# Where the scaled upper words of the weights are kept while they are rounded: a PSUM bank or their own place in SBUF

## The chip, the cores and the metric

The kernel runs on one core of a Trainium2 chip. The metric is the device time of one execution in microseconds (us), as the median of several runs. The engines of the core work side by side, each through its own queue in order: TensorE (PE, with its weight loads as PEld), VectorE (DVE), ScalarE (ACT), GpSimd (POOL) and SyncE (SP), whose queue here issues nearly all transfers. Semaphores order what one engine needs from another.

## What is computed

Eight sequences of 576 tokens go through an attention block with 8 heads of 64, then through a Fourier mixing over tokens and columns, a normalization, and a two-layer network of 512 to 2048 to 512 columns:

```python
q_s = softmax(q, axis=-1); k_s = softmax(k, axis=2)
kv = np.einsum('bhsd,bhse->bhde', k_s, v)
x = np.einsum('bhsd,bhde->bhse', q_s, kv)        # then (B,H,S,D) -> (B, S, H*D)
mixed = np.real(np.fft.fft(np.fft.fft(x, axis=1), axis=2))
u = x + mixed
un = (u - mu) / np.sqrt(var + 1e-06)
ch = np.maximum(un @ w_ch1, 0.0) @ w_ch2
return u + ch
```

The two weight matrices reach the kernel as 64-bit words, two 32-bit halves in turn, and have to be brought to float32 on the chip before TensorE can use them. This is the rounding that the change is about.

## The kernel before

**The weights.** Each of the two matrices is cut into 16 blocks of 128 x 512, 32 blocks in all, called words 0 to 31 here (0 to 15 are `w_ch1`, 16 to 31 `w_ch2`). `fetch(i)` brings a block of 64-bit words into SBUF, 128 partitions x 512 words of 8 bytes, lower and upper half in turn, so each half is a view with a step of two. The places are listed by `WORDS_AT`: parts of the large tile `big` that hold nothing yet, three tiles called `words`, and two called `spare`. `convert(i)` makes float32 of it in five steps:

1. ScalarE scales the upper half into `t` (L397).
2. DVE shifts `t` left by three bits into the block's final place in `big` (L391; word 16 goes by way of a tile `eo`).
3. DVE joins the sign of `t` to it (L394, two inputs: `t` and what step 2 wrote).
4. ScalarE scales the lower half in place (L398).
5. GpSimd adds the lower half to the joined word (L399), which is the finished block.

For words 3 to 25, 23 of them, `t` is a PSUM bank from `acc`, a pool of three banks that in this part of the kernel also takes the results of attention and mixing. For the other nine, `t` is the upper half itself, in SBUF, written in place. When step 5 is done, SP's queue fetches the next block that goes to the same place.

**The order.** Each step of the kernel has a time written out by hand, and the program sorts all steps by it; this gives the order in every engine's queue. The five steps of a word stand at offsets 0, 0.8, 1.5, 0.9 and 2.3 from its time (`converted`), so in the queues the lower half's scaling comes after the shift and before the sign pass. The times decide only the order: what starts when is up to the engines and the semaphores.

**What runs around it.** Words 0 to 2 are rounded in the opening. From about 46 us on, the first group of tokens goes through the first layer (`plain`: `half` for the first three blocks, then `up`, L1457), one block of `w_ch1` after the other, in the three banks `ba`, `bb` and `bc` in turn. ScalarE applies the ReLU to each (L1472), and a bank is filled again only after its ReLU. From about 104 us the second layer follows (`part`, L1479). Beside this run:

- the keys of the next sequence (`keys`): DVE takes four maxima (L733) and combines them across partitions with the help of ScalarE's copies (`across`: L713, L716, and DVE's L720); ScalarE then takes the exponentials (L737);
- `combine` (L449), DVE's subtractions and additions of quarters of finished blocks, two inputs in SBUF each, which are then stored to DRAM for the later groups (L452 to L458);
- the queries of the next sequence: DVE's maxima and sums (L968, L946 and others), GpSimd's subtraction (L973), ScalarE's exponential (L977), TensorE's transposes (L985) and products (L840).

From about 175 us on, the other groups run through the layers with the stored combinations (`up` and `down`, L1544, L1641, L1671), without any rounding.

Of the kernel before, what the change touches and what calls it, by code (L numbers as in the profile page):

```python
# [40 lines left out]
F32 = mybir.dt.float32  # L41
# [5 lines left out]
P = 128  # L47
B, H, S, DH = 8, 8, 576, 64
D = H * DH
# [89 lines left out]
class _Block:  # L139
# [211 lines left out]
    def weights(self):  # L351

        nc = self.nc
        w1 = self.w1.bitcast(I32).rearrange("(k p) n -> p k n", p=P)
        w2 = self.w2.bitcast(I32).rearrange("(f p) n -> p f n", p=P)
        raws = self.raws = {}

        def fetch(i):

            at = WORDS_AT[i]  # L360
            if at < 8:
                raw = self.w2sb[:, 2 * at:2 * at + 2, :].rearrange("p a n -> p (a n)")
            elif at < 11:
                raw = self.words[at - 8][:].rearrange("p a n -> p (a n)")
            else:
                raw = self.spare(2 * D)
            raw = raw.bitcast(I32)
            f = i % NF
            if i < NF:
                nc.sync.dma_start(raw.rearrange("p (k n) -> p k n", k=KT), w1[:, :, f * 2 * P:(f + 1) * 2 * P])  # L370
            else:
                nc.sync.dma_start(raw, w2[:, f, :])
            raws[i] = raw

        def convert(i):
            pair = raws.pop(i).rearrange("p (n w) -> p n w", w=2)
            lo, hi = pair[:, :, 0], pair[:, :, 1]
            f = i % NF
            out = (self.w1sb if i < NF else self.w2sb)[:, f, :]

            if 2 < i < 26:
                t = self.acc((P, D))
            else:

                t = hi.bitcast(F32)
            to = self.halves()[:, 0:D] if i == NF else out
            ti, V = t.bitcast(I32), nc.vector


            def shift():  # L390
                V.tensor_scalar(out=to.bitcast(I32), in0=ti, scalar1=3, scalar2=None, op0=ALU.logical_shift_left)  # L391

            def sign():
                V.scalar_tensor_tensor(out=to.bitcast(I32), in0=ti, scalar=-(1 << 31), in1=to.bitcast(I32),  # L394
                                       op0=ALU.bitwise_and, op1=ALU.bitwise_or)

            return [(0, lambda: nc.scalar.activation(t, hi.bitcast(F32), ACT.Copy, scale=2.0 ** -112)), (0, shift), (0, sign),  # L397
                    (0, lambda: nc.scalar.activation(lo, lo.bitcast(U32), ACT.Copy, scale=2.0 ** -29)),  # L398
                    (0, lambda: nc.gpsimd.tensor_tensor(out=out.bitcast(I32), in0=to.bitcast(I32), in1=lo, op=ALU.add))]  # L399

        return fetch, convert
# [1592 lines left out]
```

## Time and profile before

| | before |
|---|---|
| median of 3 runs, us | 1006.84 (1006.43 to 1006.99) |
| span of the profiled execution, us | 1006.6 |
| granted TensorE clock, mean | 1.000 |
| ACT busy, us | 493.2 (49%) |
| POOL busy, us | 442.9 (44%) |
| L399, all 32 adds, first and last start, us | 32.9 to 144.3 |
| L391, all 32 shifts, DVE busy, us | 20.4 |

Of the profiled execution only the span is shown, from the first instruction to the last; a time of the same execution by the device's own measure is not.

How the views read. A row of the timeline has the start in us, the duration in us, the engine, the line of the kernel, the operation, what it writes and reads, its shape and how many instructions are merged into it; in brackets stands the idle time of the engine before it, and what ended that. A row that groups a line's instructions has the least, the median and the greatest duration in ns, then the first and the last start. Two instructions of one engine may overlap by some hundredths of a us in these records. A DVE row that is long can be long because it waited inside the instruction: such time counts as busy.

### The profile page before, as it was taken

The page shows a single profiled execution, that of the slowest core. Times are in us where ns is not written, and L with a number is a line of the kernel's source. Part 1 is how long each engine was busy: PE and PEld are TensorE (multiplying, and loading weights), DVE is VectorE, ACT ScalarE, POOL GpSimd, SP SyncE. Part 2 cuts the span into 40 slices and gives each one's busy share as a digit, 9 for nine tenths or more (in the row PEclk, how much of TensorE's full clock was granted, in tenths as well). Part 3 has the DMA queues.
Part 4 walks back from the last instruction along what each step waited for, and adds up shares of the span by engine and source line. Part 5 has one row for each costly group of instructions (what it writes and reads, how often), then busy time and mean ns, then how long its engine had stood idle before and what let it go on. Part 6 is the DMA issues. An engine that isn't in the chain of part 4 may idle for free.

```text
span 1006.6 us, 19808 instructions
## 1 busy us (share of the span) xinstructions
PE 995.6 (99%) x7562; PEld 855.7 (85%) x7562; DVE 718.6 (71%) x1356; ACT 493.2 (49%) x1277; POOL 442.9 (44%) x445
## 2 busy tenths in 40 slices
PE   8999999999999999999999999999999999999998
PEld 6844464888888899889988998899889998998897
DVE  6898898666765887588756877688667945685563
ACT  4585642872468228832775177625772342151200
POOL 4263420357535637664655465655646450040000
PEclk9999999999999999999999999999999999999999
DMA  9987499687989666975677577847753765674573
GB/s 300 258 281 245 158 240 346 205 243 226 342 283 272 230 230 219 266 237 210 251 220 242 206 269 237 253 174 270 231 204 135 267 213 200 224 265 172 183 256 132
DMA packets 123559, 236.37 MB, mean 235 GB/s; under 512 B 24184, under 2 KB 88440, under 8 KB 112840
## 3 DMA queue, kind: packets, MB, share of 16 engines
q1 hardware_dynamic: 123096, 234.58, 71.0%
q8 instruction: 60, 0.98, 0.4%
q14 instruction: 35, 0.29, 0.1%
q10 hardware_dynamic: 288, 0.26, 0.1%
q0 software_dynamic: 80, 0.26, 0.1%
HBM read 199.94 MB, written 39.06 MB: 237 GB/s over the span
## 4 chain that ended last, share of the span: by engine, by line
PE 87%; DVE 7%; ACT 3%; DMA 1%; issue 1%; SPq 0%; POOL 0%; DVEq 0%; POOLq 0%
PE bb L1544 16%; PE ba L1544 11%; PE bc L1544 11%; PE bb L1671 10%; PE ba L1671 7%; PE bc L1671 7%; PE bb L1641 5%; PE bc L1479 2%; PE bb L1760 2%; PE two L840 2%; PE one L755 2%; PE two L1207 1%; PE two L1264 1%; PE ba L1479 1%; PE bc L1760 1%; PE ba L1760 1%
## 5 line engine op out<-in xcount | busy, mean ns | idle before, releaser
L1544 PE MATMUL bb<-unT,big 128*128 128x256 f32 x768 | 183.3, 380 | 0.0
L1544 PEld LDWEIGHTS bb<-unT,big 128*128 128x128 f32 x768 | 144.8, 190 | 20.7 <-DVE u L1514 0.7
L1556 ACT ACTIVATE big<-big 128x512 f32<-128x512 f32 x96 | 59.8, 629 | 147.6 <-DVE big L1555 141.0
L1544 PE MATMUL ba<-unT,big 128*128 128x256 f32 x512 | 123.9, 382 | 0.0
L1544 PE MATMUL bc<-unT,big 128*128 128x256 f32 x512 | 121.5, 380 | 0.1
L817 ACT ACTIVATE qT<-q 32x128 f32<-32x128 f32 x384 | 117.9, 307 | 5.9 <-DVE q L807 0.8
L1544 PEld LDWEIGHTS bc<-unT,big 128*128 128x128 f32 x512 | 96.9, 190 | 13.7 <-DVE big L1555 0.5
L1544 PEld LDWEIGHTS ba<-unT,big 128*128 128x128 f32 x512 | 95.5, 190 | 13.9 <-issue 0.5
L1514 DVE TENSOR_TENSOR u<-bb,s 128x512 f32<-128x512 f32 x66 | 45.2, 685 | 85.0 <-PE bb L1544 66.5
L1671 PE MATMUL bb<-big 128*128 128x128 f32 x848 | 103.8, 276 | 0.2 <-DVE u L1678 0.2
L1671 PEld LDWEIGHTS bb<-big 128*128 128x128 f32 x848 | 98.9, 192 | 1.0 <-DVE u L1678 1.0
L1390 POOL COPY unT<-unT 32x256 f32<-32x256 f32 x98 | 42.0, 428 | 90.2 <-DVE unT L1382 85.9
L1621 POOL TENSOR_TENSOR x<-x,big 128x512 f32<-128x512 f32 x45 | 60.9, 1368 | 46.0 <-DVE big L1678 19.7
L1617 DVE TENSOR_TENSOR big<-big 128x512 f32<-128x512 f32 x98 | 79.9, 842 | 0.0
L1671 PE MATMUL ba<-big 128*128 128x128 f32 x640 | 79.0, 276 | 0.0
L1671 PEld LDWEIGHTS ba<-big 128*128 128x128 f32 x640 | 75.0, 192 | 0.8
L1390 ACT COPY unT<-unT 32x256 f32<-32x256 f32 x126 | 50.7, 402 | 31.3 <-DVE unT L1382 29.5
L804 POOL TENSOR_TENSOR q<-q,qm 128x512 f32<-128x512 f32 x24 | 25.8, 1073 | 88.2 <-DVE qm L799 53.1
L405 POOL TENSOR_TENSOR big<-big 128x512 f32<-128x512 f32 x24 | 30.4, 1268 | 68.4 <-ACT big L1556 68.4
L1641 PE MATMUL bb<-big 128*128 128x256 f32 x256 | 58.3, 379 | 0.0
L1555 DVE TENSOR_TENSOR big<-bc,u 128x512 f32<-128x512 f32 x64 | 44.0, 688 | 17.3 <-PE bc L1544 16.4
L1641 PEld LDWEIGHTS bb<-big 128*128 128x128 f32 x256 | 48.0, 190 | 6.1
(336 smaller groups left out, 1917.9 us busy)
## 6 DMA issues: line engine op xcount, KB each, us to landing
big<-w2d SPq DMA_DIRECT2D x67, 1024.0 KB, 4.6
big<-w1s SPq DMA_DIRECT2D x64, 896.0 KB, 4.7
big<-w2s SPq DMA_DIRECT2D x16, 1024.0 KB, 4.8
big<-in_w_dram SPq DMA_DIRECT2D x21, 512.0 KB, 6.0
w2d<-big SPq DMA_DIRECT2D x42, 256.0 KB, 6.5
kb<-in_kT_dram SPq DMA_DIRECT2D x28, 320.0 KB, 7.8
q<-in_q_dram SPq DMA_DIRECT2D x28, 256.0 KB, 6.0
vt<-in_v_dram SPq DMA_DIRECT2D x84, 80.0 KB, 2.7
```

The costliest lines, as they stand in the source:

```text
L405: e1.tensor_tensor(out=to(4), in0=at(2), in1=at(3), op=ALU.add)
L817: nc.scalar.activation(to[t, i * Q:i * Q + Q], one, ACT.Exp)
L1390: copy(to, of)
L1514: plus = lambda t: V.tensor_tensor(out=temp(t), in0=box["bb"][:], in1=box["s1"][:], op=ALU.add)
L1544: nc.tensor.matmul(bank()[:, i, :], lhsT=w[:, WA_AT[m], k * P:(k + 1) * P], rhs=self.unT[g][:, B_AT[m], k, :], start=first and i == 0 and ...
L1555: steps = [(0, lambda: V.tensor_tensor(out=hp(i), in0=bank()[:], in1=u()[:], op=ALU.add)), (0.8, lambda: nc.scalar.activation(hp(i), hp(i) ...
L1556: (0.8, lambda: nc.scalar.activation(hp(i), hp(i), ACT.Relu))]
L1617: e.tensor_tensor(out=to(o), in0=to(x), in1=to(y), op=op)
L1621: E.tensor_tensor(out=x, in0=x, in1=tile(m), op=ALU.add)
L1641: nc.tensor.matmul(box[name][:, i, :], lhsT=h[p][:, A_AT[m], i * P:(i + 1) * P], rhs=self.stream[n][:, p, :], start=p == 0 and (m != 1 or ...
L1671: nc.tensor.matmul(box[place[n]][:, i, :], lhsT=own(m)(A_AT[n])[:, f, :], rhs=w[:, r // 2, r % 2 * P:r % 2 * P + P], start=first and f == ...
L1760: nc.tensor.matmul(bank()[:, i, :], lhsT=h[p][:, A_AT[m], i * P:(i + 1) * P], rhs=w[:, p, :], start=first and i == 0 and p == 0, stop=p == ...
```

## The change

`convert` no longer asks for a PSUM bank: for all 32 words the scaled upper half is written in place, over the upper half of the fetched block, and the shift and the sign pass read it there.

```diff
-            if 2 < i < 26:
-                t = self.acc((P, D))
-            else:
-
-                t = hi.bitcast(F32)
+            t = hi.bitcast(F32)
             to = self.halves()[:, 0:D] if i == NF else out
             ti, V = t.bitcast(I32), nc.vector
```

The five steps, their engines and their order in the queues stay as they are. For words 3 to 25 the tile `t` is another: ScalarE's L397 writes SBUF with a step of two in place of PSUM without one, and L391 and L394 read it there. The pool `acc` keeps its three banks for its other users.

## Prediction

> **What bounds the kernel now.** I read the page first, for the bound and the chain of waits, then the busy time by stage, to see where TensorE has room.
>
> ```profile
> PE 995.6 (99%) x7562; PEld 855.7 (85%) x7562; DVE 718.6 (71%) x1356; ACT 493.2 (49%) x1277; POOL 442.9 (44%) x445
> PE 87%; DVE 7%; ACT 3%; DMA 1%; issue 1%; SPq 0%; POOL 0%; DVEq 0%; POOLq 0%
> ```
> ```profile
> 46.00:58.00 12.00, 12.00 (x52) 8.94 (x51) 10.10 (x16) 10.97 (x20) 7.58 (x6) 1.00 0.79 263
> 58.00:75.00 17.00, 16.79 (x40) 7.19 (x39) 16.55 (x29) 12.93 (x30) 9.30 (x8) 1.00 0.90 308
> 75.00:112.00 37.00, 36.23 (x272) 18.10 (x271) 32.77 (x61) 21.39 (x47) 12.88 (x12) 1.00 0.67 236
> 112.00:200.00 88.00, 87.89 (x447) 54.47 (x446) 72.16 (x154) 44.65 (x118) 23.59 (x20) 1.00 0.78 239
> 200.00:1006.60 806.60, 802.23 (x6299) 733.04 (x6297) 552.70 (x1018) 379.34 (x1007) 371.71 (x363) 1.00 0.69 230
> ```
>
> The columns of the second view are the stretch, its length, then busy PE, PEld, DVE, ACT, POOL, the granted clock, the DMA share and GB/s. All 23 edited words lie between 46 and 120 us. From 46 to 200 TensorE is idle for 0 + 0.21 + 0.77 + 0.11 = 1.09 us only, so **1.1 us is the most that the change can give back**. After 200 the matmuls follow one another with 4.37 us of idle time in 806.6, so what TensorE loses early it loses for good, nearly one for one. And from 58 to 75 DVE has 0.45 us of room in 17: what is put on DVE there stays there.
>
> **The change part by part.** The durations, by operand, are min/median/max in ns:
>
> ```profile
> L391 DVE TENSOR_SCALAR big<-acc x22: 678/682/693, 48.0 to 117.6; 128x512 int32<-128x512 int32 x22
> L391 DVE TENSOR_SCALAR big<-big x4: 418/424/488, 31.6 to 137.1; 128x512 int32<-128x512 int32 x4
> L394 DVE SCALAR_TENSOR_TENSOR big<-acc,big x22: 675/691/693, 48.7 to 118.4; 128x512 int32<-128x512 int32 x22
> L394 DVE SCALAR_TENSOR_TENSOR big<-words,big x2: 691/692/692, 120.8 to 143.5; 128x512 int32<-128x512 int32 x2
> L397 ACT ACTIVATE acc<-big x17: 616/641/695, 47.3 to 117.0; 128x512 f32<-128x512 f32 x17
> L397 ACT ACTIVATE big<-big x4: 668/684/699, 27.9 to 136.4; 128x512 f32<-128x512 f32 x4
> L399 POOL TENSOR_TENSOR big<-big x20: 1285/1298/1356, 32.9 to 138.9; 128x512 int32<-128x512 int32 x20
> ```
>
> No instruction is added, removed or moved. ScalarE's scaling pass (L397) goes from 641 to 684 ns: 23 x 0.043 = 1.0 us more on an engine that is half idle, spread over 70 us; I put it at nothing on the path (it would cost at most its 0.04 each where ScalarE is late). The shift (L391) goes from 682 to 424 ns: 23 x 0.26 = 6.0 us less for DVE. The sign pass (L394) has the same length, 691 and 692. The 23 allocations of an `acc` bank go, and with them ScalarE's wait for the sign pass three banks earlier; no idle time of TensorE before 200 beyond the 1.09 us above can come from it. By these terms alone the kernel gets faster by 0 to 1.1 us.
>
> What they leave out is **GpSimd**. These rows, in order of time (start, duration, engine), show what it does to DVE:
>
> ```profile
> 119.18 1.30 POOL L399 TENSOR_TENSOR big<-big 128x512 int32<-128x512 int32 x1 [0.80 <-ACT x L1042]
> 119.66 0.70 ACT L398 ACTIVATE words<-words 128x512 int32<-128x512 uint32 x1
> 119.87 0.90 DVE L391 TENSOR_SCALAR big<-words 128x512 int32<-128x512 int32 x1 [0.82 <-ACT words L397]
> ...
> 131.01 0.42 DVE L449 TENSOR_TENSOR big<-big 128x256 f32<-128x256 f32 x1
> 131.23 1.36 POOL L399 TENSOR_TENSOR big<-big,spare 128x512 int32<-128x512 int32 x1 [7.99 <-issue]
> 131.34 1.52 DVE L449 TENSOR_TENSOR big<-big 128x256 f32<-128x256 f32 x1
> ```
>
> A shift that reads SBUF and comes while GpSimd adds takes 0.90 us in place of 0.42: it ends 0.29 after the add (119.87 + 0.90 = 120.77 against 120.48). So does a subtraction with two SBUF inputs (L449): the first, alone, takes 0.42, the second ends at 132.86, 0.27 after the add's 132.59. And the add, asked for at 131.23 while the first subtraction ran, was 0.06 longer than its median: it got in between two DVE instructions that stood back to back. So an add and such an instruction **take turns**, a held one needing its length less 0.13 after the add.
>
> The Trainium skill, page "SBUF — State Buffer", section "Who interferes with whom", states this as a lock on one port pair, taken whole, by DVE instructions in a two-port mode and by those with two SBUF inputs (the latter against GpSimd instructions that read SBUF). By it the sign pass, whose two inputs now both lie in SBUF, is held as well, and the sum is the one that follows; without it only the shift would be held. The trace agrees for shift and subtraction (0.90 and 1.52 us above); no row of before shows a sign pass held.
>
> No row shows a held sign pass with two SBUF inputs, so I bound it: free, 0.69 us (below nothing it cannot cost); held, 1.36 + 0.56. I take held, since its operands are like those of L449, the nearest row. Until now shift and sign pass were what DVE did while GpSimd added the words before:
>
> ```profile
> 48.74 0.69 DVE L394 SCALAR_TENSOR_TENSOR big<-acc,big 128x512 int32<-128x512 int32 x1
> 49.35 0.68 DVE L391 TENSOR_SCALAR big<-acc 128x512 int32<-128x512 int32 x1
> 49.57 6.59 POOL L399 TENSOR_TENSOR big<-big 128x512 int32<-128x512 int32 x5 [4.29 <-DVE big L394]
> ...
> 57.42 0.69 DVE L394 SCALAR_TENSOR_TENSOR big<-acc,big 128x512 int32<-128x512 int32 x1
> 58.02 0.81 DVE L733 TENSOR_REDUCE km<-kb 128x4 f32<-128x640 f32 x1
> 58.75 0.68 DVE L391 TENSOR_SCALAR big<-acc 128x512 int32<-128x512 int32 x1
> ```
>
> The five adds run without a gap (6.59 / 5 = 1.32), under unheld passes of 0.68 and 0.69. Now one word, from the end T of its sign pass: the next shift begins at T - 0.08 (49.35 against 48.74 + 0.69) and ends at T + 0.34; the add is asked for at T + 0.14 (49.57 against 49.43), gets in at the shift's end less 0.13, T + 0.21, and ends at T + 1.50; the next sign pass, asked for at T + 0.37, is held and ends at 1.50 + 0.56 = **T + 2.06**, where DVE needed about 1.33 to 1.4 before. Word 3 is rounded here first (L394 at 48.74), word 9 last (57.42). Word 3 has no add against it: its shift saves 0.26, but ScalarE's next pass is no earlier, so I keep only its sign pass's new end, 49.20 (48.02 + 0.04 + 0.42 + 0.03 + 0.69). Six words on: 49.20 + 6 x 2.06 = 61.56 against 57.42 + 0.69 = 58.11. DVE is **3.45 us late** at 58. What comes next decides whether TensorE sees it:
>
> ```profile
> 62.44 0.68 DVE L391 TENSOR_SCALAR big<-acc 128x512 int32<-128x512 int32 x1
> 63.37 0.81 DVE L733 TENSOR_REDUCE km<-kb 128x4 f32<-128x640 f32 x1
> 64.21 0.20 ACT L713 COPY across<-km 64x16 f32<-64x16 f32 x1 [3.75 <-DVE km L733]
> 64.65 0.60 ACT L1472 ACTIVATE big<-bb 128x512 f32<-128x512 f32 x1
> 64.91 1.36 POOL L399 TENSOR_TENSOR big<-big 128x512 int32<-128x512 int32 x1 [2.68 <-DVE big L394]
> 65.03 0.68 DVE L391 TENSOR_SCALAR big<-acc 128x512 int32<-128x512 int32 x1
> 66.35 0.16 DVE L720 TENSOR_TENSOR km<-km,across 128x16 f32<-128x16 f32 x1
> 66.55 0.20 ACT L716 COPY across<-km 32x16 f32<-32x16 f32 x1 [0.19 <-DVE km L720]
> 67.74 0.59 PE L1457 MATMUL bb<-unT,big 128*128 128x512 f32 x1
> 70.82 0.58 ACT L1472 ACTIVATE big<-bc 128x512 f32<-128x512 f32 x1
> 71.54 0.67 PE L1457 MATMUL bc<-unT,big 128*128 128x512 f32 x1 [0.21 <-ACT big L1472]
> ```
>
> Word 10's shift (58.75) meets word 9's add (61.56 + 0.14 + 1.29 = 62.99): asked for at 58.75 + 3.45 = 62.20, it ends at 62.99 + 0.29 = 63.28 and not at 59.43, 3.85 late. Word 11's shift (62.44) meets none, and its 0.26 brings 3.6. The last maximum of the keys (63.37) is 3.6 late, so ScalarE's L713 is, and the ReLU queued behind it (64.65). Word 12's shift (65.03) came under word 11's add (64.91) before too, unheld; 3.6 later the add runs to 69.9 (64.91 + 3.6 + 1.36), and the shift ends at 70.2 against 65.71, **4.5 late**. L720 behind it on DVE is 4.5 late, L716 on ScalarE waits for L720, and the ReLU of 70.82 stands behind L716 on ScalarE with no idle time between. TensorE waited for that very ReLU at 71.54, so it has no slack: it starts at 70.82 + 4.48 + 0.58 + 0.14 = 76.02, **4.5 us late**.
>
> What comes back: from 82 to 111 lie six more words.
>
> ```profile
> L391 DVE TENSOR_SCALAR big<-acc x6: 678/683/692, 82.0 to 107.3; 128x512 int32<-128x512 int32 x6
> ...
> 104.47 0.34 PE L840 MATMUL acc<-pairs,qT 64*64 64x64 f32 x8 [0.19 <-ACT xs L1080]
> 111.23 0.44 PE L985 MATMUL tr<-ident,q 128*128 128x128 f32 x2 [0.52 <-DVE q L957]
> ```
>
> There they come 3 to 7 us apart and GpSimd's add is over before the next shift, so DVE gains 6 x 0.26 = 1.6 us on the late TensorE, and TensorE's idle 0.19 and 0.52 go. Sum: 4.5 - 0.7 = **+3.8 us**. The profiled span is 1006.6 us; nothing around it is shown, and it is 0.2 from the median of 1006.84, so 1006.84 + 3.8 = **1010.6 us**.
>
> **The rivals.**
>
> *Cheaper shifts win (faster).* The sign pass is not held, or the add always finds a gap. Then one word takes about what it did, later shifts save 0.26, and TensorE regains its idle 0.21, 0.19 and 0.52: 0.9 us, 1005.9. For it: the duration rows, 424 against 682, and no held sign pass in the trace. Against: L449, with like operands, is held. It decides as soon as a sign pass under an add stays at 0.69.
>
> *Late, but not seen (no change).* DVE is 1 to 3 us late at 58 and the ReLU's wait absorbs it, or held words and cheaper shifts cancel: 1006.8. For it: the ReLU of 64.65 ends 2.5 us before TensorE begins to fill its bank again (67.74). Against: that of 70.82 has none, and DVE has 0.45 us of room.
>
> *Held to the end of the layer (much slower).* All thirteen words before 75 us meet an add, 0.73 each: 9.5 us, less 0.7, 1015.6. For it: GpSimd is busy 9.3 of the 17 us after 58. Against: words 11 and 13 to 15 come apart, behind key work that takes no turns.
>
> That the lower words' pass would now wait for the shift, both halves lying in one buffer, is excluded: at 119.66 (L398) it ran before its own shift at 119.87 (L391) had begun.
>
> **How the numbers follow.** Forecast 0.60, with 1008.5 to 1012.5 as its own range (three held words fewer or more at 0.73). Much slower 0.10, so slower 0.70; no change 0.15; faster 0.15. About 0.2% (2 us) is what a measurement of this kernel tells from no change, so the faster rival at 0.9 us would itself be hard to tell; part of its chance stands for a gain that I cannot price. The range takes in the faster rival's 1005.9 below and goes to 1014.0 above, two thirds of the way from the forecast to the third rival.
>
> **What would show it.** Right: L391 has one form of about 0.42 us where no add runs and ends 0.29 after one that does; sign passes of 1 to 1.9 us between 49 and 62; words 3 to 9 take about 12 us on DVE and not 9; the five adds no longer run without a gap; the first ReLU after ScalarE's key copies is some 3.6 us late; TensorE idles some 4.5 us between 67 and 76 and hardly anywhere else before 200. Wrong: sign passes of 0.69 throughout, or a TensorE with no new idle time before 76. If DVE is late but TensorE is not, the step from L720 to the ReLU failed; if adds wait for DVE in place of DVE for them, the turn-taking failed.

## The result, and the profile after

The changed kernel takes 1012.69 us (median of 4 runs, 1012.52 to 1014.05) against 1006.75 before: ratio 1.0062, 95% interval 1.0048 to 1.0076. In a second set of runs (`after_again` below) it was 1011.83 against 1007.00, ratio 1.0045, interval 1.0029 to 1.0062. It is slower, as forecast: the loss is 4.8 to 5.9 us where 3.8 was forecast, so the forecast of 1010.6 lies 1.2 to 2.1 us below the two medians.

The second median stands for neither half of its runs. Two of its four executions took 1013.08 and 1013.42 us, with a mean granted TensorE clock of 0.998 and 0.997; the other two took 1010.59 and 1010.50, with 1.000. In the first set all four have 0.997 or 0.998. What this clock has to do with the loss is taken up below.

The page's row of the engines, then the busy time by stage (PE, PEld, DVE, ACT, POOL, granted clock, DMA share, GB/s):

```profile
PE 996.2 (99%) x7562; PEld 855.4 (85%) x7562; DVE 721.6 (71%) x1356; ACT 494.1 (49%) x1277; POOL 444.1 (44%) x445
```
```profile
58.00:75.00 17.00, 13.14 (x31) 5.29 (x29) 16.36 (x25) 8.60 (x19) 8.65 (x7) 1.00 0.74 239
75.00:112.00 37.00, 36.43 (x236) 17.95 (x237) 33.10 (x62) 23.97 (x54) 14.40 (x12) 0.95 0.71 237
112.00:200.00 88.00, 88.00 (x459) 53.00 (x459) 72.51 (x152) 42.72 (x109) 20.57 (x17) 1.00 0.79 242
200.00:1010.70 810.70, 806.55 (x6336) 736.71 (x6332) 554.24 (x1024) 383.28 (x1020) 376.23 (x368) 1.00 0.70 230
```

The page hides the matter, since every engine's total moves by 3 us at most. The stages show it. TensorE is idle for 3.86 us between 58 and 75 where it was idle for 0.21, and between 75 and 200 by 0.57 in all; and its granted clock is 0.95 between 75 and 112, which no row of before showed.

Times differ from run to run: 19 runs of the kernel before on one chip spread over 3 us (1005.87 to 1008.88). A part of that is the kernel's opening, for in the profiles shown here block 3 begins anywhere from 52.41 to 54.40 us. So the traces are best compared over a stretch that leaves it out: **from the first matmul of block 3 to the first of the next group** (54.01 and 174.78 us in the trace before, L1457 and L1544). It is 120.77 us before and 125.44 after (53.57 to 179.01), +4.67. What follows it, to the end of the span, is 831.8 and 831.7.

This is the rounding in its dense part (start, duration, engine, line). L387 is the shift, L390 the sign pass and L395 the add; the line numbers are four lower than before:

```profile
48.09 0.69 DVE L390 SCALAR_TENSOR_TENSOR big<-big 128x512 int32<-128x512 int32 x1
48.77 0.43 DVE L387 TENSOR_SCALAR big<-big 128x512 int32<-128x512 int32 x1
48.91 1.45 POOL L395 TENSOR_TENSOR big<-big 128x512 int32<-128x512 int32 x1 [4.06 <-DVE big L390]
49.23 1.67 DVE L390 SCALAR_TENSOR_TENSOR big<-big 128x512 int32<-128x512 int32 x1
50.83 0.41 DVE L387 TENSOR_SCALAR big<-big 128x512 int32<-128x512 int32 x1
51.04 1.36 POOL L395 TENSOR_TENSOR big<-big 128x512 int32<-128x512 int32 x1 [0.68 <-ACT big L1468]
51.28 1.67 DVE L390 SCALAR_TENSOR_TENSOR big<-big 128x512 int32<-128x512 int32 x1
...
59.45 1.67 DVE L390 SCALAR_TENSOR_TENSOR big<-words,big 128x512 int32<-128x512 int32 x1
61.05 0.81 DVE L729 TENSOR_REDUCE km<-kb 128x4 f32<-128x640 f32 x1
```

Word 3's sign pass, with no add against it, takes 0.69. From word 4 on each takes 1.67: it ends at 49.23 + 1.67 = 50.90, which is 0.54 after the add's 50.36. The add in turn waits out the shift: 1.45 and 1.36 where it took 1.30. The rows come 2.05 us apart (49.23, 51.28), and GpSimd, which had no gap before, idles 0.68 between adds. (The bracket at 51.04 names a ReLU as what ended that gap. The add also needs its sign pass, which ended at 50.90, and the gap is as long for each of the next adds, most of which name L390.) Busy time misleads here: DVE counts as busy through the 0.98 us that a sign pass is held.

These rows show how the delay comes to TensorE:

```profile
66.51 0.80 DVE L729 TENSOR_REDUCE km<-kb 128x4 f32<-128x640 f32 x1
67.35 0.42 ACT L709 COPY across<-km 64x16 f32<-64x16 f32 x2 [7.25 <-DVE km L729]
67.79 0.60 ACT L1468 ACTIVATE big<-bb 128x512 f32<-128x512 f32 x1
68.17 1.52 DVE L387 TENSOR_SCALAR big<-big 128x512 int32<-128x512 int32 x1
70.33 0.17 DVE L716 TENSOR_TENSOR km<-km,across 128x16 f32<-128x16 f32 x1
70.53 0.84 ACT L712 COPY across<-km 32x16 f32<-32x16 f32 x4 [1.02 <-DVE km L716]
74.85 0.57 ACT L1468 ACTIVATE big<-bc 128x512 f32<-128x512 f32 x1
```
```profile
57.01 3.60 PE L1453 MATMUL bb<-unT,big 128*128 128x512 f32 x8
60.44 3.60 PE L1453 MATMUL bc<-unT,big 128*128 128x512 f32 x8
63.87 3.60 PE L1453 MATMUL ba<-unT,big 128*128 128x512 f32 x8
68.53 3.67 PE L1453 MATMUL bb<-unT,big 128*128 128x512 f32 x8 [1.06 <-ACT big L1468]
75.57 5.37 PE L1453 MATMUL bc<-unT,big 128*128 128x512 f32 x8 [3.37 <-ACT big L1468]
80.78 3.60 PE L1453 MATMUL ba<-unT,big 128*128 128x512 f32 x8
```

The last maximum of the keys is late, the copy L709 waits 7.25 us for it in place of 3.75, the ReLU stands behind it, and TensorE waits 1.06 us for a bank and then 3.37 for the next. The block after the second wait takes 5.37 us where the others take 3.60. The granted clock over that block is the third figure from the end:

```profile
73.50:76.91 3.41, 1.34 (x3) 0.68 (x4) 3.13 (x6) 3.40 (x9) 1.16 (x2) 1.00 0.75 265
76.91:80.32 3.41, 3.41 (x5) 1.35 (x4) 3.38 (x5) 3.41 (x10) 2.01 (x2) 0.50 1.00 355
80.32:83.73 3.41, 3.41 (x9) 1.52 (x8) 3.27 (x8) 3.41 (x10) 0.26 (x1) 1.00 1.00 302
```

The clock falls to 0.50 at 76.91, which is 1.34 us after the work has resumed, and is full again 3.41 us later. The next block begins 80.78 - 75.57 = 5.21 us after this one, where in the trace before (71.54 to 75.05) it was 3.51: 1.70 us are lost that no engine's wait shows.

### The profile page after: what moved, and what is told of

It is laid out like the page before. It is cut to its first block, busy times and chain, and to the rows that moved or that the text cites. A ratio compares the mean times of both kernels' runs of the same rounds, so it can differ in the third digit from the quotient of the medians.

```text
span 1010.7 us, 19819 instructions
## 1 busy us (share of the span) xinstructions
PE 996.2 (99%) x7562; PEld 855.4 (85%) x7562; DVE 721.6 (71%) x1356; ACT 494.1 (49%) x1277; POOL 444.1 (44%) x445
## 4 chain that ended last, share of the span: by engine, by line
PE 92%; DVE 4%; issue 1%; ACT 1%; DMA 1%; SPq 0%; DVEq 0%
PE bb L1540 16%; PE ba L1540 11%; PE bc L1540 11%; PE bb L1667 10%; PE ba L1667 7%; PE bc L1667 7%; PE bb L1637 5%; PE bc L1475 3%; PE bb L1756 2%; PE two L836 2%; PE one L751 2%; PE two L1203 1%; PE two L1260 1%; PE ba L1475 1%; PE bc L1756 1%
```

## The experiments

The theory is this. GpSimd's adds and DVE's passes with SBUF inputs take turns, the sign pass above all; seven dense words make DVE 3.5 us late; ScalarE's queue hands that on to TensorE; the long wait then costs clock. All edits are to the changed kernel. The stretch is the one defined above, with its two ends in us. The medians of before differ because each set of runs has its own.

| run | median, us | before, us | ratio (95% interval) | stretch, us |
|---|---|---|---|---|
| e1_burst_psum | 1007.43 | 1006.92 | 1.0005 (0.9996 to 1.0015) | 52.95 to 173.28: 120.33 |
| e2_burst_inplace | 1012.03 | 1006.92 | 1.0052 (1.0035 to 1.0069) | 53.41 to 177.82: 124.41 |
| e3_sign_sbuf | 1011.76 | 1006.92 | 1.0048 (1.0031 to 1.0064) | 53.77 to 178.34: 124.57 |
| e4_shift_sbuf | 1006.89 | 1006.92 | 1.0000 (0.9990 to 1.0009) | 52.78 to 172.63: 119.85 |
| after_again | 1011.83 | 1007.00 | 1.0045 (1.0029 to 1.0062) | 53.95 to 179.41: 125.46 |
| e5_no_add | 1006.04 | 1007.00 | 0.9994 (0.9985 to 1.0004) | 52.41 to 171.23: 118.82 |
| e6_warm | 1012.94 | 1007.00 | 1.0060 (1.0043 to 1.0077) | 52.88 to 179.04: 126.16 |
| e6b_warm7 | 1010.47 | 1007.22 | 1.0031 (1.0020 to 1.0042) | 53.03 to 176.80: 123.77 |
| e7_relu_early | 1010.36 | 1007.00 | 1.0033 (1.0020 to 1.0045) | 54.40 to 176.65: 122.25 |
| e10_five | 1009.82 | 1007.22 | 1.0024 (1.0015 to 1.0033) | 53.33 to 176.66: 123.33 |
| e8_late_inplace | 1006.69 | 1007.22 | 0.9995 (0.9986 to 1.0004) | 53.14 to 172.40: 119.26 |
| e9_late_relu | 1006.20 | 1007.22 | 0.9990 (0.9981 to 0.9999) | 53.02 to 171.84: 118.82 |

The stretches are one trace each, and so is the 120.77 us of before. In all thirteen comparisons (these twelve and the result) the time lies further above before's than the stretch does, or less far below it: by 0.9 to 1.5 us in eight of them, by 0.0 to 1.9 in all. Either that one trace of before has a longer stretch than is usual, or the kernel before opens faster as a rule than it did there; with no second trace of before this stays open. So a stretch compared with 120.77 is uncertain by about 1 us, and gains of that size have to be looked for in the times.

### Which words: the dense seven, or all 23

`e1_burst_psum` gives words 3 to 9 their banks back; `e2_burst_inplace` is the other half.

```diff
-            t = hi.bitcast(F32)
+            t = self.acc((P, D)) if 2 < i < 10 else hi.bitcast(F32)    # e1_burst_psum
+            t = self.acc((P, D)) if 9 < i < 26 else hi.bitcast(F32)    # e2_burst_inplace
```

> Words 3 to 9 get their PSUM banks back, words 10 to 25 stay in place. Turn-taking theory: the seven dense words are the cost; their sign passes are 0.69 us again, five adds run without a gap, and DVE is on time at 58 us. Words 10 and 12 may still have a shift held once (0.4 and 0.9 us), so TensorE waits up to 1 us longer than before at the ReLU near 71 us, less than 3 us in one piece, so its clock stays at 1.00. 1006.0 to 1007.5 us. Rival, that the cost is spread over all 23 words or comes from ScalarE's writes: 7 of 23 words undone takes back a third of the 5.9 us, about 1010.8.

> Only words 3 to 9 are in place, words 10 to 25 have their PSUM banks. Turn-taking theory: DVE is 2.9 to 3.4 us late at 58 us, nothing is added behind that, TensorE waits in two pieces, about 1 us and 2 us, and the clock falls in the second only if that piece is long enough. 1009 to 1011.5 us. Rival, spread over all words: 7 of 23, about 1008.5 at most, and sign passes of 0.69 us.

The sign passes of e1 by operand, in ns (least, median, greatest), its adds, and TensorE's one wait:

```profile
L390 DVE SCALAR_TENSOR_TENSOR big<-acc,big x7: 691/692/693, 47.7 to 56.4; 128x512 int32<-128x512 int32 x7
48.51 6.59 POOL L395 TENSOR_TENSOR big<-big 128x512 int32<-128x512 int32 x5 [4.30 <-DVE big L390]
71.55 3.67 PE L1453 MATMUL bc<-unT,big 128*128 128x512 f32 x8 [1.27 <-ACT big L1468]
```

With a bank for seven words the sign passes are 0.69 again, the five adds run without a gap, and the loss is gone: 1.0005, stretch 120.33. The shifts of words 10 and 12 are still held (1.08 and 1.52 us), and TensorE still waits 1.27 us, 0.06 more than was allowed for. With only those seven in place nearly all of the loss is there: 124.41. The time of e2, 1012.03, is above the 1009 to 1011.5 that were expected: TensorE's two waits are 0.94 and 2.48 us, and the clock falls after the second, which had been left open. The rival, a cost spread over 23 words, would have given 1010.8 and 1008.5.

### Which pass: the sign pass or the shift

In `e3_sign_sbuf` ScalarE and the shift use the bank, and the sign pass reads SBUF; in `e4_shift_sbuf` it is the other way round (its shift passes the upper half on unscaled and unshifted, so this part of the weights is left out).

```diff
+            t = self.acc((P, D)) if 2 < i < 26 else hi.bitcast(F32)    # both
-                V.scalar_tensor_tensor(out=to.bitcast(I32), in0=ti, scalar=-(1 << 31), in1=to.bitcast(I32),
+                V.scalar_tensor_tensor(out=to.bitcast(I32), in0=hi, scalar=-(1 << 31), in1=to.bitcast(I32),    # e3_sign_sbuf
...
-                V.tensor_scalar(out=to.bitcast(I32), in0=ti, scalar1=3, scalar2=None, op0=ALU.logical_shift_left)
+                V.tensor_scalar(out=to.bitcast(I32), in0=hi if 2 < i < 26 else ti, scalar1=0 if 2 < i < 26 else 3, scalar2=None, op0=ALU.logical_shift_left)    # e4_shift_sbuf
```

> For words 3 to 25 ScalarE and the shift use PSUM as before; only the sign pass reads SBUF (the unscaled upper half, which has the same sign). Turn-taking theory: the sign pass alone with its two SBUF inputs is held by the add; one word of the burst takes 1.43 + 0.56 = 1.99 us where both in SBUF take 2.05, sign passes of about 1.35 us or more in the burst, and nearly the whole loss appears: 1010.5 to 1013 us. Rival, that the shift in its faster form is what collides: no loss, 1006 to 1007.

> For words 3 to 25 the sign pass reads the PSUM bank as before; only the shift reads SBUF (it passes on the unscaled upper half, shifted by nothing; this part of the weights is left out). Turn-taking theory: shifts are held now and then, but a sign pass runs under the add, so one word of the burst takes about 1.45 us, DVE is at most 0.9 us late at 58 us, and later shifts save 0.26 each: 1005.8 to 1007.5 us. Rival, that the shift is what collides: 1010.5 to 1013.

Two words of e3, in order of time:

```profile
51.33 1.30 POOL L395 TENSOR_TENSOR big<-big 128x512 int32<-128x512 int32 x1 [0.69 <-DVE big L390]
51.83 1.34 DVE L390 SCALAR_TENSOR_TENSOR big<-big 128x512 int32<-128x512 int32 x1
53.09 0.68 DVE L387 TENSOR_SCALAR big<-acc 128x512 int32<-128x512 int32 x1
53.30 1.29 POOL L395 TENSOR_TENSOR big<-big 128x512 int32<-128x512 int32 x1 [0.68 <-ACT big L1468]
53.81 1.34 DVE L390 SCALAR_TENSOR_TENSOR big<-big 128x512 int32<-128x512 int32 x1
```

These are two words of e4, with its five adds:

```profile
48.03 7.12 POOL L395 TENSOR_TENSOR big<-big 128x512 int32<-128x512 int32 x5 [3.99 <-DVE big L390]
49.78 0.69 DVE L390 SCALAR_TENSOR_TENSOR big<-acc,big 128x512 int32<-128x512 int32 x1
50.39 0.73 DVE L387 TENSOR_SCALAR big<-big 128x512 int32<-128x512 int32 x1
51.22 0.69 DVE L390 SCALAR_TENSOR_TENSOR big<-acc,big 128x512 int32<-128x512 int32 x1
51.83 0.72 DVE L387 TENSOR_SCALAR big<-big 128x512 int32<-128x512 int32 x1
52.66 0.69 DVE L390 SCALAR_TENSOR_TENSOR big<-acc,big 128x512 int32<-128x512 int32 x1
```

In e3 the shift, reading PSUM, runs under the add at its usual 0.68 while the sign pass is held to 1.34; a word takes 1.98 us, and the loss is there, though ScalarE writes to PSUM as before the change. In e4 the sign pass runs under the add at 0.69; the shift is held, but only for the 0.3 us that the add still has, and a word takes 1.44. The time is that of the kernel before. So **it is the sign pass with both inputs in SBUF that costs**, and the faster shift is not what collides, though it too is held. That was the one price for which the trace before had no row.

### Without the adds

```diff
-                    (0, lambda: nc.gpsimd.tensor_tensor(out=out.bitcast(I32), in0=to.bitcast(I32), in1=lo, op=ALU.add))]
+                    (0, lambda: None if 2 < i < 16 else nc.gpsimd.tensor_tensor(out=out.bitcast(I32), in0=to.bitcast(I32), in1=lo, op=ALU.add))]
```

> The changed kernel without GpSimd's add for words 3 to 15 (their lower halves are left out of the weights). Turn-taking theory: with no add in the burst nothing holds DVE, one word takes about 1.1 us (0.45 + 0.61, or ScalarE's pace), DVE is early at 58 us, all of the loss goes: 1005.5 to 1007. Rival, that DVE's two-input pass in SBUF is slow by itself or ScalarE's write is: the loss stays, 1011 to 1013.

```profile
48.06 0.69 DVE L390 SCALAR_TENSOR_TENSOR big<-big 128x512 int32<-128x512 int32 x1
48.76 0.43 DVE L387 TENSOR_SCALAR big<-big 128x512 int32<-128x512 int32 x1
```

The loss is gone: 0.9994, and the stretch is 118.82, 1.95 us shorter than in the trace before the change. So the passes in SBUF are not slow by themselves (0.69 and 0.43 here); they are slow beside GpSimd. This run also says what the stretch costs when nothing holds TensorE up: it has no idle time from 46 to 200.

### The path: ScalarE's queue

`e7_relu_early` leaves DVE's work alone and moves ReLUs ahead in ScalarE's queue.

```diff
         for f, dt in ((0, 6), (1, 4.5), (2, 2.7)):
             first[f] = [(dt, lambda f=f: relu(f))]
+        for f, dt in ((4, 2.5), *((f, 0.1) for f in range(5, 10))):
+            first[f][1] = (dt, lambda f=f: relu(f))
```

> The changed kernel with the ReLUs of blocks 4 to 9 one place or more further ahead in ScalarE's queue, in front of the key copies that wait for DVE; DVE's work stays as it is. Theory of the path (late DVE, key copies, ReLU behind them, bank): DVE is still 3 to 4 us late at 62 us, but TensorE waits less than 1 us in all before 85 us and keeps its clock: 1006 to 1008. Rival, that the loss comes through the weights or the keys themselves: 1010.5 to 1013.

```profile
67.34 0.81 DVE L729 TENSOR_REDUCE km<-kb 128x4 f32<-128x640 f32 x1
71.56 3.60 PE L1453 MATMUL bc<-unT,big 128*128 128x512 f32 x8
76.73 3.67 PE L1453 MATMUL ba<-unT,big 128*128 128x512 f32 x8 [1.57 <-ACT big L1468]
```

DVE is as late as in the changed kernel (from block 3's start, 54.40, to the last key maximum, 67.34, are 12.94 us, and 12.94 there), but blocks 7 and 8 start on time and the clock is full. The stretch falls from 125.4 to 122.25, which shows the path. It was expected to fall further. Block 9 waits 1.57 us for its own ReLU, which stands behind the key exponentials, and two later waits for queries (0.43 us at 101.39 is one) come back, since a TensorE that is no longer late meets a DVE that still is. The median, 1010.36, lies above the 1006 to 1008 that were expected: of its 3.36 us over before, 1.48 are in the stretch, and no run says where the rest comes from.

### The clock

`e6_warm` fills the long wait with matmuls of 128x256 that nothing reads; `e6b_warm7` with half of them.

```diff
         def up(f):
+            if f == 8:
+                self.warm(14, 256)    # e6_warm; e6b_warm7: self.warm(7, 256)
             n = ("ba", "bb", "bc")[f % 3]
```

> The changed kernel with 14 matmuls of 128x256 that nothing reads, about 3.0 us, on TensorE ahead of the block whose bank it waits 3.4 us for. Theory that 1.7 us of the loss is the granted clock, which falls to about half after that idle stretch: the clock stays at 1.00, the eight matmuls take 3.6 us and not 5.4, and the time is 1.5 to 1.8 us below the changed kernel's, 1010.2 to 1011.2, with the ReLU no earlier. Rival, that the matmuls are long because of their operands or of other work then: no change, or up to 0.3 us more.

> As e6_warm, with half the filling: 14 of these matmuls took 6.2 us, two instructions each, and ran 2.5 us past the moment at which the bank was free; 7 of them take 3.0 us and end before it. Clock theory: the clock stays at 1.00, the eight matmuls take 3.6 us, the stretch from the first matmul of block 3 to the first of the next group is 1.7 us below the changed kernel's 125.4, at 123.7, with the ReLU as late as there; 1010 to 1011 us. Rival, that the filling only moves the slow stretch to the filling: 125.4, clock below 1.00 somewhere from 71 to 81 us.

The changed kernel ran beside e6_warm:

> The changed kernel once more, beside the next three on the same chip. Both theories: 1011.5 to 1013.

The filled wait in e6b_warm7:

```profile
71.49 3.19 PE L270 MATMUL tr<-pairs 128*128 128x256 f32 x14
75.07 3.67 PE L1455 MATMUL bc<-unT,big 128*128 128x512 f32 x8 [0.39 <-ACT big L1470]
78.58 3.60 PE L1455 MATMUL ba<-unT,big 128*128 128x512 f32 x8
```

e6_warm kept the clock at 1.00 and lost the gain again, because each of those matmuls is two instructions: 28 took 6.2 us, from 71.34 on, and block 8 began at 77.39 where its ReLU would have let it begin near 74.9. That was a mistake in the size of the filling, and the time of 1012.94 misses the 1010.2 to 1011.2 that were expected; the run says only that the clock stays up. With 14 instructions the filling ends in time, the next block takes 3.67 and the next but one begins 3.51 later. Stretch: 123.77, 1.69 below the 125.46 of the changed kernel, with DVE and the ReLU as late as there. So 1.7 us of the loss is clock, in an execution in which the clock falls.

### How the loss grows with the words

```diff
-            t = hi.bitcast(F32)
+            t = self.acc((P, D)) if 7 < i < 26 else hi.bitcast(F32)
```

Here words 3 to 7 alone are in place.

> Only words 3 to 7 are in place. Turn-taking theory: two words fewer are held than in e2_burst_inplace, at 0.72 each, so TensorE is 3.45 - 1.44 = 2.0 us late at block 8, in one piece of about 2.2 us, and block 7 starts on time. If the clock falls after that piece, the stretch is about 122.9 us, if not about 121.2 (before: 120.8; e2_burst_inplace: 124.4); 1007 to 1009.5 us. Rival, that the loss needs words 8 and 9 (the first that lie in tiles of their own): 120.8.

```profile
72.86 3.67 PE L1453 MATMUL bc<-unT,big 128*128 128x512 f32 x8 [2.20 <-ACT big L1468]
76.37 3.60 PE L1453 MATMUL ba<-unT,big 128*128 128x512 f32 x8
```

Block 8 begins 72.86 - 53.33 = 19.53 us after block 3, against 17.53 before the change: 2.0 us late in one piece of 2.20, as reckoned at 0.72 a word, and the clock does not fall. The rival, that words 8 and 9 are needed, is out. The stretch is 123.33 all the same and not 121.2, and the time of 1009.82 is 0.3 above the range. The difference comes later: TensorE is only 2.0 us late, DVE is late too, and the later waits stay, 0.39, 0.18, 0.52 and 0.35 us where they were 0.06, 0.19, 0.52 and 0.11. In the changed kernel, where TensorE is later, they vanish.

### A version that keeps the gain

`e8_late_inplace` writes only words 17 to 25 in place; `e9_late_relu` adds two ReLUs of e7.

```diff
-            t = hi.bitcast(F32)
+            t = self.acc((P, D)) if 2 < i < 17 else hi.bitcast(F32)    # both
...
+        for f, dt in ((4, 2.5), (5, 0.1)):    # e9_late_relu
+            first[f][1] = (dt, lambda f=f: relu(f))
```

> Words 17 to 25 in place, words 3 to 16 in their PSUM banks. Turn-taking theory: here adds are over before the next shift, so DVE saves 0.26 a word, TensorE's waits of 0.19 and 0.52 us near 104 and 111 us go, with the drains at each gap 0.7 to 1.3 us less: stretch 119.5 to 120.1 against 120.8, 1005.6 to 1006.3. Rival, that writing in place costs wherever it is done: 1007 or more.

> e8_late_inplace with the ReLUs of blocks 4 and 5 ahead of the key copies in ScalarE's queue, as in e7_relu_early. Theory of the path: TensorE's wait of 0.21 us at 71.5 us goes too, 0.2 to 0.4 us: stretch 119.1 to 119.8, 1005.3 to 1006.1. Rival, that ScalarE's later work (keys, words 13 and 14) is delayed by it: no better than e8_late_inplace.

e9_late_relu, by stage:

```profile
58.00:75.00 17.00, 17.00 (x41) 7.50 (x40) 16.25 (x28) 13.51 (x32) 8.43 (x7) 1.00 0.93 316
75.00:112.00 37.00, 37.00 (x276) 18.49 (x274) 33.60 (x64) 22.60 (x49) 15.06 (x12) 1.00 0.69 227
112.00:200.00 88.00, 88.00 (x455) 55.91 (x454) 73.63 (x157) 45.12 (x120) 22.04 (x19) 1.00 0.80 245
```

TensorE has no idle time left there. e8's stretch is 119.26, a little better than expected (119.5 to 120.1), and e9's is 118.82, as in the run without adds. Their times, 1006.69 and 1006.20, lie 0.4 and 0.1 us above their ranges. The ratio of e8, 0.9995, can't be told from no change; that of e9, 0.9990, interval 0.9981 to 0.9999, is a gain of 1.0 us that just clears the noise. So the place of the words counts. Where they are dense, writing in place costs 5.1 us of time and 3.6 of the stretch (e2); where they come far apart it costs nothing that can be told, and the stretch is 1.5 us shorter than in the one trace of before (e8).

## Why the prediction was right, and where it was short

- **The bound.** Right as to the place: TensorE has its new idle time between 58 and 76 alone, and what it loses there it keeps, for the rest of the kernel takes 831.7 us as against 831.8. As the most that can be gained, 1.1 us was too small, because it counts idle time alone. In e5 and e9 all five waits of the trace before (1.09 us) are gone, and the stretch is 1.95 us shorter, which is 0.17 more for each wait.
- **Cheaper shift.** Right in size (0.41 to 0.43 where nothing holds it). That it gains time by itself is not shown: in e4 and e8 the stretch is 0.9 and 1.5 us shorter than in the one trace of before, but the times are 0.0 and 0.5 us lower, within the noise.
- **The held sign pass.** Its price was taken from L449, whose operands are like its own, and it came out: the pass was to run from T + 0.37 to T + 2.06, which is 1.69, and takes 1.67. A word takes 2.05 where 2.06 was worked out. e3 and e4 show that it decides, and e5 that it is GpSimd's add that holds it. The trace thus bears out what the prediction took from the Trainium skill (page "SBUF — State Buffer", section "Who interferes with whom") for two inputs in SBUF: 1.67 beside an add, 0.69 without one.
- **3.45 us late at 58.** Word 9's sign pass ends at 59.45 + 1.67 = 61.12. This trace's block 3 begins 0.44 earlier than in the one before, so that is 3.45 late against 58.11.
- **The path.** The ReLU that was to start at 75.30 starts at 74.85, or 75.29 with the 0.44. TensorE's block 8 starts at 75.57 + 0.44 = 76.01 against 76.02: 4.47 late, as worked out. e7 shows that the path runs through ScalarE's queue.
- **What was left out.** The sum took a late TensorE to be late and nothing more. After 3.37 us without work its clock fell, and the block behind the wait cost 1.70 us more: a term of the sum that was taken as zero without being named. e6b shows it as 1.69.
- **What comes back.** Worked out as 0.19 + 0.52 = 0.7 us; it was 4.47 + 1.70 - 4.67 = 1.50. All four later waits of 0.06, 0.19, 0.52 and 0.11 went, 0.88 us of idle time, and a wait costs more than its idle time: block 7 begins 4.66 us after block 6 (63.87 to 68.53) and not 3.43 (57.01 to 60.44), so 1.23 us went for an idle time of 1.06. At 0.17 for each of four waits, an estimate from this and from e5, the other 0.7 us are accounted for.
- **The base.** The prediction put the span of 1006.6 us beside the median of 1006.84. A span here lies 1.8 us below the time of its own run (1010.7 and 1012.52), so the execution profiled before took about 1008.4, longer than any of its four timed runs (1006.43 to 1006.99). The difference of the two spans, 4.1, thus understates the loss.

With 0.88 + 4 x 0.17 = 1.56 for what comes back the sum is 4.47 + 1.70 - 1.56 = 4.6, and the stretch's loss is 4.67. The forecast came nearer to the result than its sum deserved: it left out 1.7 us of clock and counted 0.8 too little of what comes back, and these two errors cancel in part by chance.

The times ask for a little more than the stretch. Where the mean clock is 0.998 or 0.997, the loss is 5.9 us (first set) and 6.1 to 6.4 (1013.08 and 1013.42 against 1007.00); where it is 1.000, 3.5 to 3.6 (1010.50 and 1010.59). A fall like the one above lowers the mean by 1.70 / 1010 = 0.0017, more than a mean of 1.000 leaves room for. So these last two executions had none, and it is their time that the forecast of 1010.6, a sum without the clock, comes to. No trace of them was kept. They differ from the other two by 2.7 us, of which such a fall accounts for 1.7; the rest is open. About 1.2 us of the 5.9 lie outside the stretch by these traces; as said above, no run settles where.

## What to carry to other kernels

Before an operand of a VectorE instruction moves from PSUM to SBUF, look at what GpSimd does at that moment: work that shared the time with GpSimd may have to take turns with it, and the instruction that grows is the one with two inputs in SBUF, not the one whose own duration changed. Then ask which copy or activation, on a third engine, stands in line behind the late result, since that queue is where TensorE finds the delay. And price a wait of TensorE above the idle time that the profile shows (here 0.17 us more for each), and a long one with the clock as well (here 1.7 us, in those executions in which it fell).

## What the runs showed of the hardware that was not expected

- TensorE's granted clock fell to 0.50 for 3.41 us after a wait of 2.48 us (e2_burst_inplace), 2.86 (e3_sign_sbuf) and 3.37 and 3.40 (the two traces of the changed kernel), and the next eight matmuls together took 5.37 us each time. After waits of 1.06, 1.27, 1.57 and 2.20 us it did not fall (3.67). The fall comes 0.5 to 0.6 us after the work has resumed in e2 and e3, and 1.3 us in the changed kernel, so the row that shows it is not the row of the wait. The Trainium skill, page "TensorE: Matmul & The Clock Gate", section "HAM oscillation — how this bites in real kernels", warns of idle gaps of TensorE above about 3.4 us. Here 2.48 us were enough.
- A held instruction still needed most of its own time once the add was over: a sign pass of 0.69 us ended 0.54 after the add, and a shift of 0.42 ended 0.29 after it.
- The length of the wait alone does not decide. Within a trace the clock's changes lie whole multiples of 3.413 us apart (in the changed kernel at 76.91, 80.32 and 1012.16, that is 1 and 273 of them). Laid over the whole trace as marks, these multiples fall elsewhere on the program in each execution: the fall comes 23.34 us after block 3's start there and 21.49 after it in e2. In the four traces with a fall in this part of the kernel, the period between two marks that ends with it holds 2.07 to 2.86 us without work. No other such period of the fourteen traces, up to 990 us, holds more than 1.57. The wait of 2.20 us in e10_five is cut by a mark into 0.69 and 1.51:

```profile
67.94:71.35 3.41, 2.72 (x7) 0.93 (x5) 3.10 (x5) 3.32 (x8) 2.57 (x2) 1.00 0.84 291
71.35:74.76 3.41, 1.90 (x5) 0.98 (x6) 3.31 (x7) 3.41 (x9) 0.97 (x1) 1.00 0.78 243
```

So whether one and the same wait costs 1.7 us can depend on where it falls between the marks. This fits the changed kernel's two executions with a mean clock of 1.000, whose traces were not kept; it is not shown for them.
